# Seven block products for every output tile but the first, key folds on VectorE, split query transposes, one list for all steps

## The chip, the cores and the metric

The kernel runs on one core of a Trainium2 chip. The core's engines work side by side, each through its own queue in program order: TensorE multiplies matrices (PE in the profile; its weight loads are PEld), VectorE (DVE) and ScalarE (ACT) read TensorE's results from its accumulators in PSUM, GpSimd (POOL) folds arrays and issues the loads, SyncE (SP) issues stores and transposing DMAs. Sixteen DMA engines carry all transfers. The metric is the device time of one execution in microseconds, the median of several.

## What is computed

Attention over pooled keys and values, for 8 batches and 8 heads, followed by a three-way maxout layer and a projection.

```python
B, H, S, D = q.shape                      # 8, 8, 576, 64
pool = 8
Sp = S // pool                            # 72
k_p = k.reshape(B, H, Sp, pool, D).mean(axis=3)
v_p = v.reshape(B, H, Sp, pool, D).mean(axis=3)
scores = np.matmul(q, k_p.transpose(0, 1, 3, 2)) / np.sqrt(D)
attn = softmax(scores)                    # over the 72 pooled keys
x = matmul(attn, v_p).transpose(0, 2, 1, 3).reshape(B * S, H * D)   # 4608 x 512
h = np.maximum(np.maximum(x @ w1, x @ w2), x @ w3)                  # 4608 x 768
out = h @ w_out                                                     # 4608 x 512
```

## The kernel before

**Algebra.** The maximum is taken as x·w1 + max(0, x·(w2-w1), x·(w3-w1)). So the hidden layer has two products with difference weights (`sub_w`, line 331), and x·w1·w_out is one product with a 512x512 matrix `wm` made on the core (`turn_w`, `linear`, lines 338 to 355). An output tile then sums ten rows of 128 terms: four of `wm` with x, six of `w_out` with h.

**Tiles.** The 4608 tokens are cut into nine tiles of 512, numbered 0 to 8 (`NB`). A batch has 576 tokens, so tile n needs parts of one or two batches. For a batch b the steps are: load q, k, v (on POOL's queue, cast to 16 bits); fold eight keys into one and eight values into one; transpose queries (`qT`) and keys (`kz`); nine or eight score products with exponentials (`s`); five chunks of values (`v`: eight matmuls of 65 columns, a reciprocal and a multiplication on VectorE); five transposes of the normalised tokens into `xT` (`x`).

**Two ways to multiply.** A hidden or output tile is made directly (`hidden_part`, line 357, 48 matmuls of 512 columns; `project`, line 400, 40 of 512 columns), or as a 2x2 block product by seven instead of eight block products (`seven`, line 753, 84 matmuls of 256 columns; `out_seven`, line 643, 70 of 256). The seven need sums and differences of blocks of both operands (S1 to S4 of the weights, T1 to T4 of the tokens or hidden rows), and more than one eviction of each accumulator. The table `PRODUCTS` says which operands each of the products 1 to 7 takes. Before the change, hidden tiles 6, 7 and 8 and output tiles 2, 3, 4, 7 and 8 are made by seven products, the others directly.

**Order.** The program issues steps in an order written out by hand, and each engine's queue follows it. Three parts: `block(0, ...)`, line 810, runs tile 0's hidden layer, the product `wm` and tile 0's output, with batch 1's attention put into numbered slots. Then `MIDDLE` (line 881 and on) has a list for each of tiles 1 to 4: hidden pieces `h`, scores `s`, sums `a`, `b`, then output products, values and token transposes, with folds of the next batches on POOL (`k4+1`: one of three steps of batch 4's keys). After tile 5's hidden layer, `ORDER` (line 846) weaves the rest. Tile 8's output is made last, with the last pieces of tile 6's output behind it.

**Engines and queues.** Keys and values are folded on POOL in three additions each (`fold_steps`, lines 157 to 164; batch 0 by matmuls, batch 1's keys on VectorE). Queries of batches 3 to 7 are transposed by one DMA each on SP's queue (line 302), tokens of these batches by one DMA per chunk there (line 253); stores of the output use the same queue (lines 425 and 662). Batches 1 and 2 use TensorE for these transposes. A `!` in a list makes the next POOL fold wait for the last block sum on VectorE.

**PSUM.** In the first two parts two buffers of two banks (`att`) hold scores and values, three (`pw`) hidden and output products, one (`tr`) transposes. In the third part the tags are `val`, `sc`, `pa`, `bc` and `po`.

Of the kernel before, what the change touches and what calls it, by code (L numbers as in the profile page):

```python
# [14 lines left out]
def kernel(  # L15
# [26 lines left out]
    NG = 9  # L42
# [22 lines left out]
    kts, vts, qbs, kps, qTs, ets = {}, {}, {}, {}, {}, {}  # L65

# [15 lines left out]
    def load_v(b, eng, dtype=F16, cuts=(0, H)):  # L82
        if b == 0:
            vts[0] = ld.tile([96, 4096], dtype, name="vt0", tag="vt")[:, 0:3072].rearrange(
                "p (h i d) -> p h i d", h=H, i=6)
            src = v[0].rearrange("h (p i) d -> p h i d", i=6)
            return [eng.dma_start(out=vts[0][:, h:g], in_=src[:, h:g])
                    for h, g in zip(cuts, cuts[1:])][-1]
# [54 lines left out]
    vp_all = const.tile([Sp, B, H, 65], F16, name="vp", tag="vp")  # L143
# [10 lines left out]
    def fold(e, t, out, dtype=F32):  # L154
        return list(fold_steps(e, t, out, dtype))

    def fold_steps(e, t, out, dtype=F32):
        part, n = t.shape[:2]
        f = const.tile([part, n, 4, D], dtype, name="half" if dtype == F32 else "halfh",
                       tag="half" if dtype == F32 else "k16")  # L160
        yield e.tensor_tensor(out=f, in0=t[:, :, 0:4, :], in1=t[:, :, 4:8, :], op=ALU.add)  # L161
        yield e.tensor_tensor(out=f[:, :, 0:2, :], in0=f[:, :, 0:2, :],  # L162
                              in1=f[:, :, 2:4, :], op=ALU.add)
        yield e.tensor_tensor(out=out, in0=f[:, :, 0, :], in1=f[:, :, 1, :], op=ALU.add)

    def new_kp(b):
        kps[b] = sb2.tile([96, 6, D], BF16, name="kp", tag="kp")

    def fold_k(b, e, i0=0, i1=6):
        if b not in kps:  # L170
            new_kp(b)
        fold(e, kts[b][:, i0:i1], kps[b][:, i0:i1], F16 if e is nc.vector else F32)

    def fold_v(b):
        fold(nc.gpsimd, vts[b], vp_all[:, b, :, 0:D])

    def pool_v(b, h, g, tag, evac):

        pvp = psum([128, g - h, D], F32, name="pvp", tag=tag[0], bufs=tag[1])
        for i in range(6):  # L180
            nc.tensor.matmul(pvp, pick[:, i, :], vts[b][:, h:g, i, :],
                             start=(i == 0), stop=(i == 5))
        evac(out=vp_all[:, b, h:g, 0:D], in_=pvp[0:Sp])
# [12 lines left out]
    def keys(b, tag):  # L196
        pkt = psum([128, 3, 96], BF16, name="pkt", tag=tag[0], bufs=tag[1])
        for i in range(3):
            nc.tensor.transpose(pkt[:, i, :],
                                kps[b][:, 2 * i:2 * i + 2, :].rearrange("p i d -> p (i d)"),  # L200
                                ident[0:96, 0:96])
        return pkt

    def turn_k(b):
        pkt = keys(b, ATT if len(pools) < 3 else SC)
        for par, evac in enumerate((nc.vector.tensor_copy, nc.scalar.copy)):
            for odd in range(2):
                (evac if b > 2 else nc.vector.tensor_copy)(
# [55 lines left out]
    def values(b, c0):  # L264
        tag = (ATT0, ATT, ("val", 1))[len(pools) - 1]
        pav = psum([128, 2, 512], F32, name="pav", tag=tag[0], bufs=tag[1])
        for h in range(H):
            nc.tensor.matmul(  # L268
                pav[:, h // 4, 65 * (h % 4):65 * (h % 4) + 65],
                ets[b][:, h, c0:c0 + 128], vp_all[:, b, h, :],  # L270
# [20 lines left out]
    def do(b, steps):  # L291
# [3 lines left out]
        for name in steps.split():  # L295
            i = int(name[1:] or 0)
            if name[0] in "qQ":
                turn_q(b, *QS[i], nc.vector.tensor_copy if name[0] == "Q"
                       else nc.scalar.copy, TR)
            elif name[0] == "T":  # L300
                qTs[b] = sb2.tile([128, 2 * NG, 128], BF16, name="qT", tag="qT")
                nc.sync.dma_start_transpose(
                    out=qTs[b], in_=qbs[b].rearrange("p hp t d -> p (hp t d)"))
            elif name[0] == "k":
                turn_k(b)
            elif name[0] == "K":
                fold_k(b, nc.vector)
# [7 lines left out]
            elif name[0] == "S":  # L315
                next(out_sums, None)
# [7 lines left out]
            else:  # L324
                turn_x(b, *CHUNKS[i], xns[b, i], TR if b == 1 else ATT,
                       nc.vector.tensor_copy if name[0] == "X" else nc.scalar.copy)
# [73 lines left out]
    def project(n):  # L400
        hT = hTs[n]
        for mm in range(4):
            m = 4 * n + mm
            last = m == TOK // 128 - 9
# [3 lines left out]
            for c in ((slice(0, C // 2), slice(C // 2, C)) if last else (slice(0, C),)):  # L408
                tag = PW if len(pools) < 3 else PA if last else PO
                po = psum([128, c.stop - c.start], F32, name="po", tag=tag[0], bufs=tag[1])  # L410
                for kc in range(KCH):
                    nc.tensor.matmul(po, tokens(128 * m, 128 * m + 128)[:, kc], wm_sb[:, kc, c],  # L412
                                     start=(kc == 0), stop=False)
                yield
                for jc in (0, 3, 1, 4, 2, 5):
                    nc.tensor.matmul(po, hT[:, jc, bass.ts(mm, 128)], wo_sb[:, jc, c],  # L416
                                     start=False, stop=(jc == JCH - 1))
                if c.start:
                    nc.vector.tensor_copy(out=osb[:, c], in_=po)
                else:  # L420
                    nc.scalar.copy(out=osb[:, c], in_=po)  # L421
                for u in range(2):
                    b, g = divmod(2 * m + u, NG)
                    dst = out[S * b:S * b + S, :].rearrange("(r g) c -> r g c", g=NG)
                    (nc.scalar if last and u else nc.sync).dma_start(
                        out=dst[:, GS[g], c], in_=osb[64 * u:64 * u + 64, c])
# [90 lines left out]
    def block(n, plan, parts):  # L517

        for slot, _ in enumerate(part for stage in parts for part in stage(n)):
            for b, steps in plan.get(slot, ()):  # L520
                if b < B:
                    do(b, steps)
# [3 lines left out]
    PA, BC, PO = ("pa", 2), ("bc", 1), ("po", 1)  # L526
    FIRST = {1: (0, 0), 2: (1, 2), 7: ("S3", "T3")}
    PRODUCTS = FIRST | {3: ("S4", 3), 4: (3, "T4"), 5: ("S1", "T1"), 6: ("S2", "T2")}
    sw = {}

    LEAD = {0: [(6, "s0")], 1: [(6, "s1")], 2: [(6, "s2")], 3: [(6, "s3")],
            4: [(6, "s4")], 5: [(6, "s5")], 6: [(6, "s6")], 7: [(6, "s7")],
            8: [(6, "v0 x0")], 9: [(6, "v1 x1")]}

    def minus(out, a, b):
        gate[:] = [nc.vector.tensor_tensor(out=out, in0=a, in1=b, op=ALU.subtract)]

    def fold_w(wi):
# [3 lines left out]
        tag = ("w1T", "mw0")[wi - 1]  # L542
        s = const.tile([128, 4, 2, 128 * JH], F16, name=f"sw{wi}", tag=tag)
        sw[wi] = dict(zip(range(4), a)) | {f"S{i + 1}": s[:, i] for i in range(4)}
        nc.vector.tensor_tensor(out=s[:, 0], in0=a[2], in1=a[3], op=ALU.add)
        yield
        minus(s[:, 2], a[0], a[2])
        yield
        minus(s[:, 1], s[:, 0], a[0])
        yield  # L550
        minus(s[:, 3], a[1], s[:, 1])
        yield

    def halves(n):

        return {i: tokens(NB * n + HALF * (i % 2), NB * n + HALF * (i % 2) + HALF,
                          2 * (i // 2), 2 * (i // 2) + 2) for i in range(4)}

    def turns(n):
        return (pad3 if n % 2 else pad)[:, 0:4]  # L560

    def fold_t(e, x, t):
        for i, a, b in ((0, x[1], x[0]), (1, x[3], t[0]), (2, x[3], x[1]), (3, x[2], t[1])):
            e.tensor_tensor(out=t[i], in0=a, in1=b, op=ALU.subtract)  # L564

    def fold_x(n):

        x, t = halves(n), turns(n)
        late = n >= LAST - 1
        for part in ([slice(0, 1), slice(1, 2)] if late else [slice(0, 2)]):  # L570
            fold_t(nc.gpsimd if late else nc.vector,
                   {i: x[i][:, part] for i in x}, [t[:, i, part] for i in range(4)])
        return {f"T{i + 1}": t[:, i] for i in range(4)}

    LAST = TOK // NB - 1
    th, so_new, tt_all, gate, held = {}, [], [], [], []

    def out_w(z, r0, r1):

        i, j = divmod(z, 2)  # L580
        c = slice(HALF * i, HALF * i + HALF)
        return (wm_sb[:, 2 * j + r0:2 * j + r1, c] if r1 <= 2
                else wo_sb[:, JH * j + r0 - 2:JH * j + r1 - 2, c])

    def out_s(z):
        return so_new[0][:, z - 1]

    def fold_out(r0, r1):

        if not so_new:  # L590
            so_new.append(const.tile([128, 4, 5, HALF], F16, name="so", tag="ktTrue"))
        w = [out_w(z, r0, r1) for z in range(4)]
        t = [None] + [so_new[0][:, z, r0:r1] for z in range(4)]
        for out, x, y, op in ((t[1], w[2], w[3], ALU.add), (t[2], t[1], w[0], ALU.subtract),
                              (t[3], w[0], w[2], ALU.subtract),
                              (t[4], w[1], t[2], ALU.subtract)):
            gate[:] = [nc.vector.tensor_tensor(out=out, in0=x, in1=y, op=op)]
            yield

    out_sums = (x for rows in ((0, 2), (2, 5)) for x in fold_out(*rows))  # L600

    def sums_of(n, name):

        t = tt_all[0]
        h = name[0] == "b"
# [374 lines left out]
```

## Time and profile before

| what | value |
|---|---|
| median of 3 runs | 226.42 us (226.37 to 226.68) |
| the profiled execution: whole run | 228.01 us |
| the profiled execution: span from first to last instruction | 226.3 us |
| granted TensorE clock | 1.00 |
| DVE group L276, scaling of values, x40 | 27.7 us, 692 ns each |
| DVE group L769, maximum of two hidden halves, x18 | 13.3 us, 754 ns each |
| POOL group L161, first addition of values, x7 | 28.4 us, 4061 ns each |
| POOL group L161, first addition of keys, x6 | 18.7 us, 3125 ns each |
| DVE group L161, the same for batch 1's keys, x1 | 0.9 us, 947 ns |
| ACT group L208, copies of transposed keys, x10 | 4.8 us, 478 ns each |
| DMA queue of POOL, share of 16 engines | 48.1% |
| DMA queue of SP and ACT, share of 16 engines | 33.0% |

Busy time of an engine is the union of its instructions' durations. Matmuls overlap and their ends are modelled, so a busy TensorE can still lose time between instructions; the distance between starts of neighbouring pieces tells what one costs.

### The profile page before, as it was taken

What the parts mean: (1) busy time and instruction counts of PE and PEld (TensorE: products, weight loads), DVE (VectorE), ACT (ScalarE), POOL (GpSimd) and SP (SyncE); (2) the same over time, 40 slices, a digit from 0 to 9 for tenths busy, and PEclk for the clock granted to TensorE, in tenths of its full rate; (3) what the DMA queues carried; (4) which work ended last, traced back from release to release, by engine and by line L of the source; (5) the groups of instructions that cost most, each with busy time, mean ns of one, the idle gap of its engine ahead of it and who ended that gap; (6) DMA issues with size and microseconds to landing.
All of it is one profiled execution on the core that took longest, in us unless ns stands there. A gap on an engine that the chain in (4) does not pass through costs nothing.

```text
span 226.3 us, 4691 instructions
## 1 busy us (share of the span) xinstructions
PE 214.7 (95%) x1807; PEld 146.4 (65%) x1807; DVE 148.6 (66%) x292; ACT 122.3 (54%) x221; POOL 138.6 (61%) x111
## 2 busy tenths in 40 slices
PE   6788999999999999999999999699999999999993
PEld 2467745558656555965686568355677677788882
DVE  3668876038595385876679668535668886898840
ACT  2267524755874577238624862475687446555330
POOL 7974300999949967787677758999500913872020
PEclk9999999999999999999999999999999999999999
DMA  6999999989759999659999599965241534200265
GB/s 167 210 197 197 208 207 208 203 163 224 128 106 191 217 220 208 112 129 151 199 226 191 31 216 236 182 126 132 58 107 29 122 61 95 46 3 0 55 203 164
DMA packets 47351, 33.54 MB, mean 148 GB/s; under 512 B 27041, under 2 KB 42337, under 8 KB 47329
## 3 DMA queue, kind: packets, MB, share of 16 engines
q0 software_dynamic: 16944, 16.98, 48.1%
q1 hardware_dynamic: 29936, 15.87, 33.0%
q10 hardware_dynamic: 448, 0.39, 0.7%
q8 instruction: 14, 0.23, 0.5%
q14 instruction: 9, 0.07, 0.1%
HBM read 34.60 MB, written 9.44 MB: 195 GB/s over the span
## 4 chain that ended last, share of the span: by engine, by line
PE 69%; DMA 15%; POOL 11%; issue 1%; DVE 1%; ACT 1%; POOLq 0%
PE pw L362 21%; PE oA L713 9%; DMA vt<-in_v_dram 8%; PE pA L789 7%; PE po L416 7%; PE po L412 5%; PE oC L713 4%; PE psc L218 4%; DMA mw<-in_moe_w_dram 4%; PE pC L789 3%; POOL half L161 3%; DMA xT<-xn 3%; PE pav L268 3%; PE oB L713 2%; POOL half L162 2%; PE pB L789 2%
## 5 line engine op out<-in xcount | busy, mean ns | idle before, releaser
L362 PE MATMUL pw<-xT,mw 128*128 128x512 f16 (+1 forms) x336 | 72.8, 348 | 1.9 <-DMA xT<-xn 1.6
L362 PEld LDWEIGHTS <-mw 128*128 128x128 f16 x336 | 31.6, 98 | 22.3 <-DMA xT<-xn 1.8
L370 DVE TENSOR_TENSOR hT<-t,pw 128x512 f16<-128x512 f16 (+1 forms) x42 | 25.4, 609 | 25.1 <-ACT et L223 17.8
L223 ACT ACTIVATE et<-psc 72x576 f16<-72x576 f32 (+2 forms) x54 | 35.2, 661 | 6.8 <-PE psc L218 6.7
L161 POOL TENSOR_TENSOR half<-vt 72x2048 f32<-72x2048 f16 x7 | 28.4, 4061 | 13.8 <-DMA vt<-in_v_dram 13.3
L162 POOL TENSOR_TENSOR half<-half 72x1024 f32<-72x1024 f32 (+1 forms) x13 | 27.3, 2098 | 11.0 <-DVE rcp L274 6.1
L368 ACT ACTIVATE t<-pw 128x512 f16<-128x512 f32 (+1 forms) x42 | 22.5, 537 | 16.2 <-PE pw L362 15.8
L276 DVE TENSOR_TENSOR xn<-pav,rcp 128x512 f16<-128x512 f32 x40 | 27.7, 692 | 1.4
L416 PE MATMUL po<-mwo,hT 128*128 128x512 f16 (+1 forms) x102 | 23.5, 366 | 0.0
L218 PE MATMUL psc<-qT,kz 128*128 128x320 bf16 (+2 forms) x120 | 22.4, 278 | 0.8 <-DVE qT L194 0.6
L218 PEld LDWEIGHTS <-kz 128*128 128x128 bf16 x143 | 13.1, 98 | 13.3 <-ACT qT L194 1.1
L161 POOL TENSOR_TENSOR half<-ktFalse 96x1536 f32<-96x1536 f16 x6 | 18.7, 3125 | 4.0 <-issue 2.9
L564 POOL TENSOR_TENSOR pad<-xT 128x256 f16<-128x256 f16 x8 | 5.9, 732 | 22.5 <-ACT pad L795 13.9
L795 ACT CAST pad<-pA 128x512 f16<-128x512 f32 x27 | 15.6, 588 | 7.2 <-PE pA L789 7.0
L268 PEld LDWEIGHTS <-et 72*128 72x128 f16 x320 | 15.1, 98 | 3.6 <-issue 0.4
L723 ACT COPY osb<-oA 128x512 f32<-128x512 f32 x12 | 7.0, 586 | 19.2 <-PE oA L713 19.2
L274 DVE RECIPROCAL rcp<-pav 128x8 f32<-128x8 f32 x40 | 8.2, 204 | 14.0 <-PE pav L268 13.6
L412 PE MATMUL po<-wm,xT 128*128 128x512 f16 (+1 forms) x68 | 16.6, 366 | 0.0
L268 PE MATMUL pav<-vp,et 72*128 72x65 f16 x320 | 16.4, 194 | 0.1
L421 ACT COPY osb<-po 128x512 f32<-128x512 f32 (+1 forms) x16 | 9.2, 573 | 12.0 <-PE po L416 12.0
L789 PEld LDWEIGHTS <-sw 128*128 128x128 f16 x144 | 13.7, 98 | 2.5
L766 DVE TENSOR_TENSOR pad<-pad,pC 128x512 f16<-128x512 f16 x18 | 12.3, 685 | 3.9 <-PE pC L789 3.6
(122 smaller groups left out, 380.0 us busy)
## 6 DMA issues: line engine op xcount, KB each, us to landing
out_dram<-osb SPq DMA_DIRECT2D x38, 128.0 KB, 5.5
ktFalse<-in_k_dram POOLq DMA_DIRECT2D x7, 576.0 KB, 8.2
qb<-in_q_dram POOLq DMA_DIRECT2D x7, 576.0 KB, 13.0
vt<-in_v_dram POOLq DMA_DIRECT2D x7, 576.0 KB, 17.5
mw<-in_moe_w_dram POOLq DMA_DIRECT2D x9, 256.0 KB, 9.4
out_dram<-osb SPq DMA_DIRECT2D x8, 256.0 KB, 7.4
ktTrue<-in_k_dram SPq DMA_DIRECT2D x3, 384.0 KB, 5.2
out_dram<-ob SPq DMA_DIRECT2D x8, 128.0 KB, 2.6
```

Source lines behind the costliest of these rows:

```text
L161: yield e.tensor_tensor(out=f, in0=t[:, :, 0:4, :], in1=t[:, :, 4:8, :], op=ALU.add)
L162: yield e.tensor_tensor(out=f[:, :, 0:2, :], in0=f[:, :, 0:2, :], in1=f[:, :, 2:4, :], op=ALU.add)
L218: nc.tensor.matmul(out, kz_all[b % 2][f % 2][rows, h, :], qTs[b][rows, n + i0:n + i1, 64 * (h % 2):64 * (h % 2) + 64], start=True, stop=True)
L223: nc.scalar.activation(out=out, in_=in_, func=FT.Exp, scale=1.0 / 64.0)
L268: nc.tensor.matmul(pav[:, h // 4, 65 * (h % 4):65 * (h % 4) + 65], ets[b][:, h, c0:c0 + 128], vp_all[:, b, h, :], start=True, stop=True)
L276: nc.vector.tensor_tensor(out=xn, in0=pv[:, :, :, 0:D], in1=rcp.to_broadcast([128, 2, 4, D]), op=ALU.mult)
L362: mm = nc.tensor.matmul(pw, w_sb[wi][:, kc, bass.ts(jc, 128)], x[:, kc], start=(kc == 0), stop=(kc == KCH - 1))
L370: nc.vector.tensor_tensor(out=hT[:, jc, c0:c1], in0=t, in1=pw, op=ALU.max)
L412: nc.tensor.matmul(po, tokens(128 * m, 128 * m + 128)[:, kc], wm_sb[:, kc, c], start=(kc == 0), stop=False)
L416: nc.tensor.matmul(po, hT[:, jc, bass.ts(mm, 128)], wo_sb[:, jc, c], start=False, stop=(jc == JCH - 1))
L713: nc.tensor.matmul(p, left, right, stop=(r == 4), skip_group_check=True, start=(i in FIRST and r == 0 and (m == 0 or n == LAST)))
L789: mm = nc.tensor.matmul(p[:, w], a[:, kc, bass.ts(g, 128)], b[:, kc, :], start=(i in FIRST and w + kc == 0), stop=(w + kc == 2), skip_grou ...
```

## The change

**Output tiles.** Tiles 1 to 7 are made by `out_product`, which takes any of the seven products by itself; tile 8 by `out_last`; tile 0 stays direct (`project`). Hidden tiles 6, 7 and 8 stay with seven products (`hidden_product`), 1 to 5 direct (`two_products`; tile 1 in halves of 256 tokens).

**Product 1 and 2.** Before, product 1 was copied to SBUF and VectorE added product 2 to it. Now product 1 is copied from its bank A into a fresh bank B, product 2 is accumulated onto it by TensorE, and the result is read once. In the hidden layer the upper half of rows then takes a ReLU on ScalarE and a maximum on VectorE of 256 columns each.

**Evictions.** `move` puts a copy on ScalarE, or on VectorE where the step's name in the list has a `*`.

**Keys and values.** Keys of batches 1 to 7 are folded on VectorE in two additions to two halves `[96, 2, 6, D]`; the third addition is made by TensorE, which accumulates both halves in six matmuls with the identity in place of three transposes. Batch 1's values are pooled by twelve matmuls with `pick`; those of batches 2 to 7 on POOL in four pieces, then two, and a last addition on VectorE. Each POOL piece waits for the last instruction listed as `shared`, a sum on VectorE.

**Queries.** Each DMA transpose of queries is in three parts of six blocks.

**Sums.** All sums of tokens (`t`) and hidden rows (`u`) are on VectorE, in every tile that uses them. Before, those of tokens of tiles 7 and 8 and part of tile 7's hidden rows were on POOL.

**Scores and PSUM.** After the first block all scores are in nine pieces of 512 columns (`scores_flat`). Four single banks `pb0` to `pb3` are handed out in turn (`take`, `give`) to all hidden and output products; `sc` (2) holds scores and transposes, `val` (one buffer of two banks) the values.

**Order.** One list holds everything after tile 0's hidden layer and the weight product. Letters: `p` half a step of tile 0's output, `s31` score piece 1 of batch 3, `v31` and `x31` its value chunk and transpose, `T3` a third of its query transpose, `K3`, `V3` pieces of its folds, `<k3` a load, `A1` `A2` the two weight products of hidden row block A (of A, B, C, D, E, H) of the next direct tile, `A3` `A4` its two halves in tile 1, `1a` product 1 of hidden row group a of a seven-product tile, `1d` product 1 of an output tile, `t`, `u` block sums, `f` `F` `S` `G` weight sums, `k3` the transposed keys, `P0` pooling of batch 1's values.

```diff
+    def move(out, in_):
+        (nc.vector.tensor_copy if on_vector[0] else nc.scalar.copy)(out=out, in_=in_)
...
-        kps[b] = sb2.tile([96, 6, D], BF16, name="kp", tag="kp")
+        kps[b] = sb2.tile([96, 2, 6, D], F16, name="kp", tag="kp")
...
         for i in range(3):
-            nc.tensor.transpose(pkt[:, i, :],
-                                kps[b][:, 2 * i:2 * i + 2, :].rearrange("p i d -> p (i d)"),
-                                ident[0:96, 0:96])
+            for j in range(2):
+                nc.tensor.matmul(pkt[:, i, :], kps[b][:, j, 2 * i:2 * i + 2, :].rearrange("p i d -> p (i d)"),
+                                 identh[0:96, 0:96], start=(j == 0), stop=(j == 1))
...
                 nc.sync.dma_start_transpose(
-                    out=qTs[b], in_=qbs[b].rearrange("p hp t d -> p (hp t d)"))
+                    out=qTs[b][:, 6 * i:6 * i + 6],
+                    in_=qbs[b].rearrange("p hp t d -> p (hp t d)")[:, 768 * i:768 * i + 768])
...
+    free_banks = [0, 1, 2, 3]
+    taken = {}
+
+    def take(key, shape=(128, 2, 256)):
+        i = free_banks.pop(0)
+        taken[key] = i, psum(list(shape), F32, name="pb", tag=f"pb{i}", bufs=1)
+        return taken[key][1]
+
+    def give(key):
+        free_banks.append(taken.pop(key)[0])
...
+    def hidden_product(n, i, g):
...
+        if i == 1:
+            move(out=bank("B", n, g), in_=p)
+        elif i in (6, 5):
+            move(out=y[:, i == 5], in_=p)
+        elif i in (2, 3):
+            t0 = sb2.tile([128, NB], F16, name="t0", tag="t0")[:, 0:HALF]
+            nc.scalar.activation(out=t0, in_=p[:, 0], func=FT.Relu)
+            nc.vector.tensor_tensor(out=h_of(g)[:, i - 2], in0=t0, in1=p[:, 1], op=ALU.max)
+        if i in (5, 7) and (n, 12 - i, g) in done:
+            plus(1)
+        if i == 4:
+            plus(0)
+            shared[:] = [nc.vector.scalar_tensor_tensor(
+                out=h_of(g + JH), in0=y[:, :, 0], scalar=0.0, in1=y[:, :, 1],
+                op0=ALU.max, op1=ALU.max)]
...
+    def out_product(n, i):
+
+        p = bank(of(i), n, "d")
+        for r in range(5):
+            for m in range(2):
+                nc.tensor.matmul(p[:, m], *out_operands(n, i, m, r), stop=(r == 4),
+                                 start=(i in (1, 7) and r + m == 0), skip_group_check=True)
...
+        if i == 1:
+            move(out=bank("B", n, "d"), in_=p)
+        elif i != 4 and i != 7:
+            move(out=o(int(i in (5, 3)))[:, :, lo if i in (2, 3) else hi], in_=p)
...
+        f = const.tile([Sp, H, 4, D], F32, name="half", tag="half")
+        e = nc.gpsimd
+        for i in range(0, H, 2):
+            c = slice(i, i + 2)
+            yield e.tensor_tensor(out=f[:, c], in0=t[:, c, 0:4, :], in1=t[:, c, 4:8, :],
+                                  op=ALU.add)
...
+        gate = shared[0]
+        op = next(folding[what, b])
+        if op is not None and gate is not None:
+            after([op], gate)
...
+    ORDER = """
+        q10* k1 p q11* q12* P0 q13* s10 K2 <k3 s11 p* s12 s13 <k4 p s14 P1 s15 V2 s16 s17 K2
+        s18 p v10 q20 q21* p k2 V2 f G v11 x10* p* v12 V2 V2 <v3 K3 G x11 s20 <q3 p q22 v13
+        K3 F s21 p* s22 s23 D3 V2 s24 q23* C3 V2 x13 K4 <q4 T3 V2 x12 A3 S v14 s25 t1 s26 F
+        C4 s27 s28 B4 k3 v20 x14 B3 E4 v21 K4 x20 t2 H3 A4 x21 v22 E3 V3 H4 k4 T3 x22* v23
+        <k5 V3 V3 t1 T4 D4 T3 F B1 u1 V3 S B2 t3 s30 s31 H1 s32 G V3 v24 s33 H2 u3 C1 C2 <k6
+        1d* V3 s40 K5 S G <v4 u2 s41 S <q5 T4 A1 s34 A2 f s35 E1 s36 T4 s37 V3 6d* u4 s38 E2
+        s42 K5 s43 K6 5d* u1 v30 s44 x23 2d x24* s45 D1 v31 f k5 s46 V4 3d t2 v32 K6 7d t4
+        s47 s48 T5 v33 D2 k6 <q6 t3 4d V4 1d t1 V4 D1 T5 T5 u2 D2 t4 V4 V4 v34 V4 E1 6d* C1
...
+        4b 5d 4a 1c 3d 6c* t1 7d u4 5c t2 2c 7c 3c 4d 1a v72 4c 6a u1 1b 2a 5a v73 6b u2 2b
+        3a t3 5b v74 1d u4 u3 3b 7a 6d t4 2d* 1c 4a 5d* 2c t1 6c 7d t2 7b t3 3d* 4d 5c 4b 1a
+        3c 7c 2a 6a 1b 4c t4 5a 6b 7a 2b 3a 5b 4a u1 1d 3b 7b 2d 1c u2 u3 4b 6d* 6c 2c u4 7c
+        5c 5d* 3c 7d 4c 3d 4d
+    """
+
+    run(ORDER)
+    last = out_last(LAST)
+    for i in range(4):
+        sum_h(LAST, i)
```

More of the change, by code (lines that the diff above doesn't have):

```diff
@@ L559, in turns @@
[L559 to L573, printed above, removed]
@@ new lines, in fold_out @@
+    def fold_out(h, e):
+        if h:
+            s = const.tile([128, 4, JH, HALF], F16, name="soh", tag="w1T")
+        else:
+            s = sums[:, 3072:5120].rearrange("p (i k c) -> p i k c", i=4, k=2)
+        so[h] = s
+        w = [out_w(z, h) for z in range(4)]
+        yield both(s[:, 0], w[2], w[3], ALU.add, e)
+        yield both(s[:, 2], w[0], w[2], ALU.subtract, e)
+        yield both(s[:, 1], s[:, 0], w[0], ALU.subtract, e)
+        yield both(s[:, 3], w[1], s[:, 1], ALU.subtract, e)
```

667 lines of the change are left out of this document (276 added, 391 removed), and 3 rows, old and new, of the table stop.

## The prediction

> **What bounds the kernel now.** I read four views: the page's busy row and slices, busy time by stretch, the chain of waits, and single groups. TensorE first.
>
> ```profile
> PE 214.7 (95%) x1807; PEld 146.4 (65%) x1807; DVE 148.6 (66%) x292; ACT 122.3 (54%) x221; POOL 138.6 (61%) x111
> ...
> PE   6788999999999999999999999699999999999993
> ```
>
> PE is busy 95% of the span. Its slices fall only in the first 20 us, in slice 26 (141 to 147 us) and in the last slice. By stretch (length, then busy us and instructions of PE, PEld, DVE, ACT, POOL, then clock, DMA share, GB/s):
>
> ```profile
> 57.00:78.00 21.00, 20.86 (x167) 12.11 (x165) 12.19 (x25) 13.54 (x26) 17.66 (x10) 1.00 0.83 158
> 78.00:99.50 21.50, 21.35 (x177) 14.49 (x176) 15.81 (x33) 11.97 (x21) 16.16 (x10) 1.00 0.90 163
> 121.00:143.00 22.00, 21.44 (x179) 14.27 (x177) 16.19 (x34) 11.61 (x20) 15.56 (x10) 1.00 1.16 162
> 143.00:158.50 15.50, 13.91 (x93) 7.52 (x91) 6.81 (x13) 9.26 (x16) 14.95 (x8) 1.00 0.77 149
> 158.50:180.00 21.50, 21.50 (x197) 15.36 (x195) 16.00 (x32) 14.56 (x28) 7.41 (x8) 1.00 0.34 73
> 180.00:200.00 20.00, 20.00 (x169) 15.23 (x168) 15.88 (x25) 11.09 (x21) 9.38 (x14) 1.00 0.32 68
> 222.00:226.30 4.30, 0.49 (x5) 0.20 (x2) 0.42 (x1) 0.00 (x0) 0.00 (x0) 0.99 0.51 141
> ```
>
> The part that is already one woven list (158.5 on) has no idle PE; the part by stages (36 to 158.5) loses a little in each and 1.6 us in one place. The chain of waits (start, length, what) names that place:
>
> ```profile
> 137.42 1.09 PE oC L713 x10
> 138.71 6.32 DMA xT<-xn
> 145.17 1.02 PE pw L362 x4
> ```
>
> TensorE waits for transposed tokens. In the timeline, SP's queue holds two token transposes from 137.3, then one whole query transpose (4.94 us from 140.08), and only then three more. Two rows matter later: the time from issue to landing of the 27 token transposes, and a vector subtraction (min/median/max ns) that once took 1348.
>
> ```profile
> DMA to landing us min/median/max: 2.3/2.7/11.8
> ```
>
> ```profile
> L597 DVE TENSOR_TENSOR so<-wm x2: 417/882/1348, 62.3 to 64.0; 128x512 f16<-128x512 f16 x2
> ```
>
> So TensorE's own work, plus what it loses between 37 and 158, sets the time.
>
> **Work moved on or off TensorE.** From starts of neighbouring pieces in the chain: a 512-column matmul costs 0.2165 us (four in 0.86), a 256-column one 0.109 (ten in 1.09), eight value matmuls 0.27 (sixteen are busy 0.69, eight 0.42). An output tile done directly is 40 x 0.2165 = 8.66 us, by seven products 70 x 0.109 = 7.63. Tiles 1, 5 and 6 change over: 3 x -1.03 = **-3.1**. Keys go from 3 transposes to 6 matmuls in each of 7 batches: 21 x 0.042 (three pkt are busy 0.29, of which some 0.165 is the tail of the last) = **+0.9**. Values of batch 1 go through twelve `pick` matmuls instead of GpSimd: 12 x 0.109 = **+1.3**. Scores change their cut, not their columns: 0. Net **-0.9 us**.
>
> **Waits that the list could remove.** From 37.7 (end of the weight product) to 158.3 lie 120.6 us. Counted by kind: hidden layers of tiles 1 to 5, 216 x 0.2165 + 48 x 0.109 = 52.0; tiles 0 and 1 out, 17.3; tiles 2 to 4 out, 22.9; scores of six batches at 1.95, 11.7; 27 value steps, 7.3; query, key and token transposes, 4.8. Together 116.0, so **4.6 us** are lost there; the windows show 2.9 of it as idle, and the rest hides under modelled ends of matmuls. The new list starts attention of batches 1 and 2 beside tile 0's output, and puts other products between each wait and its user. The split query transposes stop one 4.9 us block from holding token transposes. Upper bound of this gain 4.6, lower bound 0.
>
> **What else moves, at no cost while PE covers it.** DVE: sums of tokens and hidden rows, now in all eight tiles, 32 x 0.42 + 32 x 0.557 = 31.3 against 16.6 now, +14.6. Key folds 6 x (0.947 + 0.555), rows of batch 1's fold, +9.0. Last step of six value folds, +2.5 (0.42 each, as other 512-element f16 adds). Sixteen output and two hidden evictions put on DVE, 18 x 0.687, +12.4; three of tile 0 and nine query and token copies, less two of now, +5. Two more output adds +1.6. Key copies to ACT -8.6. Hidden products -5.0: per group five DVE passes of 0.69 to 0.75 become three of these and two 256-column maxima of 0.416, because product 1 is written into a second bank and product 2 accumulates on it. In all about +31, so 149 becomes 180 of some 223 us. GpSimd falls from 139 to some 66: 24 x 1.03 + 12 x 1.19 for folds (4.06/4 and 2.35/2), 25 for loads, the rest set-up. ACT stays near 122: -18 evictions, +13.4 key copies, more hidden passes.
>
> DVE is the cover to distrust. Over the last four full lines of the list (about 155 to 204 us) I count 49.1 us of DVE durations beside 49.1 of PE. But a DVE instruction that doesn't read its forerunner starts about 0.084 before that one's end (subtractions of 0.55 start every 0.47 in the timeline at 134.92); with that it is 42.8, or 87%, and 97% in the worst line. It fits, with little slack: no cost in the sum, up to +1.5 in the range.
>
> At the start of the list DVE meets the fold of batch 2's keys, whose load landed at 45.1; the copy of tile 0's first output, the second fold and batch 1's value steps queue behind it. From 45.1 to the end of line 3 DVE has 2.2 + 7.1 + 6.3 = 15.6 us to do (overlapped starts), which ends at 60.7; PE's own work reaches that point at 58.1. Line 4 asks 7.3 of DVE beside 9.9 of PE, so DVE catches up there. PE waits only where a value step needs the bank that DVE has not read (the second and third of batch 1, by this walk): 0.5 us in all, part of the new waits below. POOL's loads leave in the old order up to 25 us, later ones earlier than now (batch 5's keys near 62, against 78.9), each as its buffer comes free. SP carries 15 query transposes in place of 5; whole ones took 1.95 to 5.5 us there, so thirds should take 0.7 to 1.8; SP is empty more than half the time.
>
> [...] The subtraction of 1348 ns started at 62.28, while GpSimd added from 62.08 to 63.34; the same form alone takes 417. [...] More such DVE instructions (some 70 against 44 while GpSimd folds) run beside shorter GpSimd pieces. [...] If each of 36 pieces held up one sum by half its 1.1 us, DVE would gain 20 us: its 91 us on lines 1 to 14 (102.6 of durations, less the 0.084 where starts overlap) would be 111 beside 117 of PE. [...]
>
> **The end.** Now PE stops at 222.5, then one 0.42 copy and two 64 KB stores on two queues, 3.8 us. After, the last vector add is followed by two 128 KB stores on SP: some 0.5 later, from 2.6 (128 KB) against 2.1 to 2.3 (64 KB) to land: **+0.5**; bounds 0 and 1.
>
> **New waits.** Bounds: 0, as in the woven stretch of before, and 7.6 (rival 2). I take **+2.0**, the rate of the steady stage, whose repeat of 21.72 us holds 21.45 of counted work: 0.27 in 21.7, over 180 us of list 2.2; the 0.5 of the early loads is in it.
>
> **Sum.** 226.3 - 0.9 - 4.6 + 0.5 + 2.0 = 223.3 of span. The median of runs, 226.42, is 0.1 above the span (the profiled run itself took 228.01 with what lies around it): **223.4 us**, own range 221.2 (no new wait) to 225.3.
>
> **Rivals.**
> [...]
> 2. *Token transposes land late: slower.* 18 of 27 landed in 2.3 to 3.7 us, nine took 4.2 to 11.8, all with loads of k, q, v in flight. The tightest place in the list is tile 3's first product (first D1 of that tile): 5.1 us of PE work lie between the value step v32 and it. The step's two vector passes take 0.93, so the transpose must land within 4.2 of issue. At the median of the slow nine (8.0) PE waits 3.8, at 11.8 it waits 7.6: 227.2, up to 231. Against: the loads before it are listed some 12 us earlier and should have landed.
> 3. *Nothing is won back*: the 4.6 us are lost again in other places, at the early loads and in the DVE-full end: 226.3 - 0.9 + 0.5 + 0.5 = 226.4. It costs the same as rival 1 and shares its chance.
>
> **Chances.** Forecast 0.61, rivals 1 and 3 together 0.14, rival 2 0.25. A difference under 0.2%, 0.45 us, can't be told from none here. The forecast lies wholly below 225.97; of the 0.14 I put 0.03 faster, 0.08 same, 0.03 slower; rival 2 slower. So faster 0.64, same 0.08, slower 0.28. The range takes in the list without waits and part of rival 2: 220.8 to 228.6.
>
> **What would show it.** Right: PE busy near 214 of a span of 223; no PE stall over 1 us between 40 and 215; no token transpose on the chain ahead of tile 3; POOL near 66, DVE near 175. Wrong: sums with medians over 0.5 us (rival 1); a DMA xT<-xn piece of several us in the chain (rival 2); ACT or PE waiting on DVE after 155 (the DVE count); PE idle around 40 to 60 above 1.5 us (early loads).

## The result, and the profile after

| what | before | after |
|---|---|---|
| median, device us | 226.55 | 235.44 (234.32 to 237.28) |
| ratio, with its 95% interval | 1 | 1.040 (1.030 to 1.050) |
| profiled span | 226.3 | 234.7 |
| last matmul ends | 222.5 | 230.2 |
| granted clock, mean | 1.00 | 0.993 |

The change makes the kernel 4.0% slower; 223.4 us and a faster kernel were forecast. The busy rows and slices of the page after (each digit is the busy share of a fortieth of the span, in tenths):

```profile
PE 216.5 (92%) x1985; PEld 161.0 (69%) x1986; DVE 171.4 (73%) x353; ACT 121.5 (52%) x238; POOL 73.5 (31%) x84
...
PE   7787998999999999679997969999999999999992
...
PEclk9999999999999999979999999999999999999999
```

PE's work is not what grew: 216.5 us busy against 214.7, with part of that at a lower clock. New are three holes, in slices 17, 22 and 24 of 40 (digits 6, 7 and 6; these slices begin at 94, 123 and 135 us), with the clock down in slice 18, behind the first. The windows of the changed kernel (bounds, length, busy us and instructions of PE, PEld, DVE, ACT, POOL, then clock, DMA share, GB/s) say when:

```profile
80.00:100.00 20.00, 17.60 (x179) 13.47 (x177) 15.99 (x33) 15.02 (x29) 5.13 (x6) 1.00 0.94 141
100.00:120.00 20.00, 18.76 (x155) 12.55 (x156) 12.50 (x26) 7.76 (x14) 9.61 (x9) 0.91 0.93 150
120.00:140.00 20.00, 16.26 (x129) 9.79 (x127) 12.56 (x25) 8.31 (x15) 7.57 (x9) 1.00 0.99 173
140.00:160.00 20.00, 20.00 (x190) 14.60 (x189) 15.27 (x30) 10.21 (x21) 10.34 (x9) 1.00 0.89 152
...
101.00:103.00 2.00, 1.76 (x6) 0.76 (x7) 0.90 (x2) 0.43 (x1) 1.27 (x1) 0.71 1.14 336
103.00:105.00 2.00, 2.00 (x13) 0.97 (x12) 0.65 (x2) 0.17 (x1) 0.13 (x1) 0.50 0.88 195
...
200.00:222.00 22.00, 22.00 (x202) 19.49 (x200) 19.75 (x37) 9.90 (x21) 0.00 (x0) 1.00 0.21 50
```

From 140 to 222 TensorE is never idle, not even where VectorE is 90% busy (19.75 of 22). The chain of waits (start, length, what) names all three holes:

```profile
92.78 0.69 DVE xn L268
...
93.50 7.60 DMA xT<-xn
...
101.24 3.00 PE pb L664 x8
...
117.06 7.37 DMA qT<-qb
...
124.46 0.33 PE psf L210 x2
...
128.93 8.18 DMA qT<-qb
...
137.16 0.49 PE psf L210 x4
```

Each is a transposing DMA that takes 7 to 8 us. The timeline of TensorE puts the stop behind each in brackets: 3.64, 1.31 and 2.43 us.

```profile
101.24 3.00 PE L664 MATMUL pb<-xT,mw 128*128 128x512 f16 x8 [3.64 <-DMA xT<-xn]
124.46 0.33 PE L210 MATMUL psf<-qT,kz 128*128 128x320 bf16 x2 [1.31 <-DMA qT<-qb]
137.16 0.49 PE L210 MATMUL psf<-qT,kz 128*128 128x256 bf16 x4 [2.43 <-DMA qT<-qb]
```

With no load in flight, 15 token transposes of this kernel landed 2.3 to 4.8 us after issue, their median 2.4, and four thirds of query transposes 2.8 to 4.5. The timeline of POOL's queue shows what left beside the first:

```profile
93.41 0.77 POOL L104 DMA_DIRECT2D qb<-in_q_dram  x1
```

Load q6 landed at 101.28, the two parts of the token transpose at 101.10 and 101.45. The second hole is T6's middle third (117.06 to 124.42) beside load k7 (117.27 to 123.63); the third is its last third (128.93 to 137.12) beside v6 (129.13 to 138.39) and q7.

**Where the time went.** The forecast's own sum puts the last matmul, without any waits, at 222.5 - 0.9 - 4.6 = 217.0. At the prices of the prediction I walked the list and took, for each step of TensorE, its start in the trace less the list's work before it. This *lag* creeps up by 0.4 us in each of the two long stretches without such a wait, so its jumps are the losses:

| place | us |
|---|---|
| start of the list to s17 (q12 +0.75, s10 +0.38, s17 +0.39) | 2.8 |
| from there to v32 | 0.4 |
| first D1 of tile 3 waits for tokens | 3.8 |
| lower clock behind it | 1.6 |
| T6, middle third | 1.5 |
| T6, last third | 2.6 |
| from 140 to the end | 0.4 |
| sum, lag of the last matmul | 13.1 |

The forecast allowed 2.0 of it. The rest, 11.1, and a tail of 4.6 instead of 4.3 make up 234.7 - 223.3 = 11.4.

### The profile page after: what moved, and what is told of

It is laid out like the page before. It is cut to its first block, busy times and chain, and to the rows that moved or that the text cites. A ratio compares the mean times of both kernels' runs of the same rounds, so it can differ in the third digit from the quotient of the medians.

```text
span 234.7 us, 5073 instructions
## 1 busy us (share of the span) xinstructions
PE 216.5 (92%) x1985; PEld 161.0 (69%) x1986; DVE 171.4 (73%) x353; ACT 121.5 (52%) x238; POOL 73.5 (31%) x84
## 4 chain that ended last, share of the span: by engine, by line
PE 74%; DMA 14%; DVE 5%; ACT 2%; issue 1%; POOL 1%; SPq 1%; POOLq 0%; DVEq 0%
PE pb L706 19%; PE pb L664 14%; PE pb L615 12%; DMA qT<-qb 7%; PE psf L210 5%; PE pb L655 4%; PE pw L352 4%; DMA vt<-in_v_dram 4%; PE pav L260 3%; DMA xT<-xn 3%; PE pb L747 2%; PE pm L339 2%; PE pb L403 2%; DVE xn L268 2%; PE pxt L251 1%
## 5 line engine op out<-in xcount | busy, mean ns | idle before, releaser
L664 PE MATMUL pb<-xT,mw 128*128 128x512 f16 x192 | 48.3, 388 | 3.6 <-DMA xT<-xn 3.6
L796 POOL TENSOR_TENSOR half<-vt 72x512 f32<-72x512 f16 x24 | 28.3, 1193 | 53.5 <-DVE xs L526 19.4
L215 ACT ACTIVATE et<-psf 72x512 f16<-72x512 f32 x63 | 34.7, 588 | 19.4 <-PE psf L210 19.3
L664 PEld LDWEIGHTS <-mw 128*128 128x128 f16 x192 | 18.1, 99 | 20.2 <-issue 5.3
L671 DVE TENSOR_TENSOR hT<-t,pb 128x512 f16<-128x512 f16 (+1 forms) x36 | 21.2, 595 | 12.4 <-PE pb L664 9.8
L669 ACT ACTIVATE t<-pb 128x512 f16<-128x512 f32 (+1 forms) x36 | 18.7, 526 | 21.5 <-PE pb L664 15.8
L210 PE MATMUL psf<-qT,kz 128*128 128x256 bf16 (+4 forms) x161 | 21.6, 249 | 4.4 <-DMA qT<-qb 3.7
L210 PEld LDWEIGHTS <-kz 128*128 128x128 bf16 x185 | 14.2, 97 | 10.7 <-issue 5.3
L800 POOL TENSOR_TENSOR vt<-half 72x512 f16<-72x512 f32 x12 | 15.0, 1262 | 12.6 <-DVE hs L526 6.0
L706 PEld LDWEIGHTS <-hs 128*128 128x128 f16 x168 | 16.4, 98 | 1.9
L266 DVE RECIPROCAL rcp<-pav 128x8 f32<-128x8 f32 x40 | 8.1, 202 | 12.7 <-PE pav L260 12.6
L706 PE MATMUL pb<-soh,hs 128*128 128x256 f16 x126 | 17.2, 273 | 0.0
```

What stands on the lines that cost most here:

```text
L210: nc.tensor.matmul(out, kz_all[b % 2][f % 2][rows, h, :], qTs[b][rows, n + i0:n + i1, 64 * (h % 2):64 * (h % 2) + 64], start=True, stop=True)
L215: nc.scalar.activation(out=out, in_=in_, func=FT.Exp, scale=1.0 / 64.0)
L664: nc.tensor.matmul(a, w_sb[part + 1][:, kc, bass.ts(j, 128)], tokens(NB * n, NB * n + NB)[:, kc], start=(kc == 0), stop=(kc == KCH - 1))
L669: nc.scalar.activation(out=relus[j], in_=a, func=FT.Relu)
L671: nc.vector.tensor_tensor(out=hTs[n][:, j, c], in0=relus[j], in1=b, op=ALU.max)
L706: nc.tensor.matmul(p[:, m], *out_operands(n, i, m, r), stop=(r == 4), start=(i in (1, 7) and r + m == 0), skip_group_check=True)
```

## The experiments

The theory: a transposing DMA that is issued while loads are in flight lands with them, and the new list has too little work between such a transpose and its user. Rivals: the split of the query transposes alone, or the list itself (engines, copies, PSUM banks). All runs start from the changed kernel unless said otherwise; ratios are to the kernel before.

**1. One late load moved, one group of transposes moved, both** (e1, e2, e3).

```diff
# e1_q6_later
-        s47 s48 T5 v33 D2 k6 <q6 t3 4d V4 1d t1 V4 D1 T5 T5 u2 D2 t4 V4 V4 v34 V4 E1 6d* C1
+        s47 s48 T5 v33 D2 k6 t3 4d V4 1d t1 V4 D1 T5 T5 u2 D2 t4 V4 V4 v34 V4 <q6 E1 6d* C1
# e2_t6_early (the two later T6 are taken out)
-        ... u3 V5 v40 T6 2d* u4 ...
+        ... u3 V5 T6 T6 T6 v40 2d* u4 ...
```

> The changed kernel with one load moved: batch 6's queries are listed behind the sixth piece of batch 4's value fold instead of ahead of its second. Theory (a token transpose issued beside a 576 KB load lands with the load): the two transposes that tile 3's first product needs land within 4 us of issue instead of 7.6; the 3.8 us wait ahead of that product goes, and with it the stretch of lower granted clock behind it (1.6 us): about 5.4 us less, 230.0 us. Rival (SP's queue or the transposing itself is slow there, whatever POOL loads): the wait stays, 235.4 us.

> The changed kernel with batch 6's three query transposes listed together ahead of value step v40, none behind it. Theory: their two waits (1.5 us at score piece s62, 2.6 us at s64 and s65), each behind a transpose issued within 0.2 us of a load, go: 4.1 us less, 231.3 us. Rival (the waits only move to the token transposes that now stand behind the three on SP's queue): 235 us, with TensorE waiting for xT<-xn around tile 4.

> Both edits of the two runs beside this one. Theory: the gains add, 5.4 + 4.1 = 9.5 us less, 226 us, level with the kernel before, and no wait over 1 us for a transposing DMA. Rival (one wait hides another): less than 7 us gained, 228.5 us or more.

Measured: e1 238.92 us, 1.050 (1.043 to 1.057); e2 233.75, 1.027 (1.019 to 1.034); e3 237.15, 1.046 (1.041 to 1.051). All three totals missed: e1 and e3 by 9 and 11 us, e2 by 2.4 (its profiled execution, 231.46, is the shortest of its four). In e1 the wait at D1 is gone: the same transposes left at 93.77 and 94.99 and landed 2.3 us later. But T5's middle third (104.00 to 110.81) now met q6, and its last third, issued at 105.55, met q6 and v5 and landed with v5 at 118.2; TensorE stopped 3.5 and 3.7 us for them, and the granted clock of that execution averaged 0.969, against 0.993 of the changed kernel's. The long DMA at that place in e1's chain, and in e3's:

```profile
105.55 12.69 DMA qT<-qb
```

```profile
104.36 11.45 DMA qT<-qb
```

In e2 the two waits for T6 are gone as expected, and the last matmul ends at 225.0 instead of 230.2, the earliest of the three. Yet T6's thirds met a load again: issued at 108.40, 109.67 and 111.66 beside v5 (108.22 to 116.62), they took 7.8 to 8.4 us, only now TensorE did not wait for them. In e1 and e3 a load moved off one transpose lands on the next.

**2. TensorE kept busy through the wait** (e4): sixteen matmuls of 512 columns ahead of D1, whose product nobody reads.

```diff
-        ... 1d t1 V4 D1 T5 T5 u2 ...
+        ... 1d t1 V4 W16 D1 T5 T5 u2 ...
```

> The changed kernel with 16 more matmuls of 512 columns on constants, 3.5 us of work, where TensorE idles ahead of tile 3's first product; their result is used nowhere. Theory (the granted clock falls because TensorE idled for 3.6 us): the clock stays at 1.00 there, the following products run at their usual 0.2165 us, and the kernel is 1.6 us faster in spite of more work: 233.8 us. Rival (the clock falls for another reason): same time or up to 3.5 us more, the clock still low after 101 us.

Measured: 242.2 us, 1.064 (1.056 to 1.071). In the profiled execution, at 244.55 us the longest of four, T6's last third fell on loads v6 and q7 later on (11 us); what lengthened the other three is not shown. But at D1 the question is answered, by the windows of e4 at that place:

```profile
100.00:102.00 2.00, 1.35 (x7) 0.50 (x6) 0.30 (x1) 0.00 (x0) 0.00 (x0) 1.00 0.37 127
102.00:104.00 2.00, 2.00 (x18) 1.05 (x17) 0.89 (x3) 0.60 (x1) 1.40 (x1) 1.00 1.17 290
```

The clock stays at 1.00, where the changed kernel showed 0.71 and 0.50; the lag grows by 4.3 there and no more, against 3.8 + 1.6. So the 1.6 us at this place are the clock's answer to the stop of 3.64 us. In e2 it stood at 0.50 too, from 101 to 103 us, behind a stop of 2.18:

```profile
98.00:100.00 2.00, 0.00 (x0) 0.01 (x1) 0.00 (x0) 0.50 (x1) 0.11 (x1) 1.00 1.21 235
100.00:102.00 2.00, 1.98 (x6) 0.74 (x7) 0.89 (x2) 0.20 (x1) 1.39 (x1) 0.54 1.16 316
102.00:104.00 2.00, 2.00 (x14) 1.04 (x13) 0.42 (x1) 0.39 (x1) 0.00 (x0) 0.60 1.22 93
```

**3. Load q6 first; then the keys of batch 1 on the other engine** (e5, e6).

```diff
# e5_q6_first, with e2's edit; <q6 taken out of its old place
-        ... s36 T4 s37 V3 6d* u4 ...
+        ... s36 T4 s37 <q6 V3 6d* u4 ...
# e6_k1_vector, on top of e5
-        q10* k1 p q11* q12* P0 q13* ...
+        q10* k1* p q11* q12* P0 q13* ...
```

> The changed kernel with batch 6's queries loaded about 11 us earlier (listed before batch 4's value fold, right after the last query transpose of batch 4, so that nothing loads beside token transposes x32 and x33 or the last thirds of batch 5's queries), and batch 6's three query transposes listed together ahead of v40. Theory (a transposing DMA issued while loads are in flight lands with the last of them): all three waits and the lower clock go, 235.4 - 3.8 - 1.6 - 4.1 = 225.9 us, a shade under the kernel before. Rival (such waits turn up elsewhere whatever is moved, because the DMA queues are full at that stage): 231 us or more.

> The run beside it, and the four copies of batch 1's transposed keys on VectorE instead of ScalarE. Theory (ahead of 47 us ScalarE, with four key copies and then exponentials, holds up TensorE: 0.75 us at q12, 0.4 at s10, 0.4 at s17): 1.2 to 1.5 us less than the run beside it, 224.5 us. Rival (the wait there is for loads): no change.

Measured: e5 235.04 us, 1.037 (1.034 to 1.039): D1 loses 0.5 instead of 3.8, and T5 meets v5 (issued 104.47) for 5.8 at s53. That is the rival of its expectation, by its time and by the wait elsewhere; that the queues are full there is not shown. e6 235.83, 1.043 (1.040 to 1.046): nothing gained. q12 waits for a PSUM bank that four key copies hold for 1.95 us on ScalarE (e5) and 1.94 on VectorE (e6).

**4. The parts alone, in the kernel before** (e7, e8).

```diff
# e7_before_split: query transposes in three parts between the token transposes
-            1 v0 x0 2 v1 x1 6:T 6 7 v2 x2 5 v3 x3 v4 x4 3 4
+            1 v0 x0 2 v1 x1 6:T0 6 7 v2 x2 6:T1 5 v3 x3 6:T2 v4 x4 3 4
# e8_before_v7: load v7 behind the token transpose that waited at 145
-            h k k7< q7< v7< h ...    1 v0 x0 2 v1 x1 7:T ...
+            h k k7< q7< h ...        1 v0 x0 2 v1 x1 v7< 7:T ...
```

> The kernel before with one part of the change alone: query transposes in three parts, with token transposes between the thirds. Reading of the prediction (one 4.9 us block on SP's queue holds the tokens for which TensorE waits at 145): 1.5 us less, 224.9 us. Rival (those two token transposes were issued ahead of the block, at 137.3 and 138.7, and landed with the load of batch 7's values, 144.2): no change, 226.5 us.

> The kernel before with the load of batch 7's values listed behind the second token transpose of batch 5 instead of ahead of all, the rest unchanged. Theory (transposes land with the loads in flight): the two transposes land 2.5 us after issue, the wait at 145 goes, 1.5 us less, 224.9 us. Reading of the prediction (the block of the query transpose): no change, 226.5 us.

Measured: e7 took 227.7 us in one run and 233.8 to 234.4 in three, so its ratio stays open; the profile, of one of the three, shows TensorE stopped for tokens (96.60 to 103.36) that met load v5 (80.99 to 102.36), 4.5 us and some 2.6 more at a lower clock (0.84 on average from 99.5 to 121). T5's last third, issued at 106.14 beside q6, landed only at 117.52, but TensorE did not wait for it. None of the four is below the kernel before, so no gain of the split alone is seen. e8: 227.45, 1.003 (1.002 to 1.005). The two token transposes landed in 4.1 and 3.2 us instead of 7.3 and 6.3, so load v7 made that wait, not the query transpose behind them. Between the two profiled executions the last matmul moves from 222.5 to 221.4. The median gains nothing: the execution of the kernel before that was profiled, 228.01 us, is 1.6 longer than the median, and whether the others had this wait at all is not shown.

**5. The split undone** (e9): each query transpose whole, where its first third was listed.

```diff
-                nc.sync.dma_start_transpose(
-                    out=qTs[b][:, 6 * i:6 * i + 6],
-                    in_=qbs[b].rearrange("p hp t d -> p (hp t d)")[:, 768 * i:768 * i + 768])
+                    nc.sync.dma_start_transpose(
+                        out=qTs[b], in_=qbs[b].rearrange("p hp t d -> p (hp t d)"))
```

> The changed kernel with each query transpose whole again, at the place where its first part is listed; everything else as changed. Theory (a transposing DMA that is issued beside a load lands with the load, so later parts have more chances to meet one): the two waits for the last parts of batch 6's queries (+1.5 and +2.6 us in the changed kernel) go, the wait of 3.8 us for tile 3's tokens and the lower clock behind it (+1.6) stay, so 235.4 - 4.1 = 231.3. Rival (it is the list's DMA traffic, not the parts): the whole transposes meet loads as the parts did, or hold the token transposes behind them by some 5 us, and the time stays at 234 to 238.

Measured: 233.97 us, 1.031 (1.027 to 1.035), at the lower edge of the rival. So the parts are not the whole cause. In the profiled execution, at 239.11 us the longest of four, the waits for T6 are gone, but batch 4's transpose, whole, left at 70.18, met a load of keys (70.36 to 80.80) and landed at 85.32; s40 lost 5.7. Whether the other three lost this too is not shown.

**6. Every transpose of batches 3 to 6 away from the loads as they stood** (e10), with batch 1's key copies shared by two engines (e11).

```diff
# e10_clear_of_loads, on top of e5
-        ... 3d t2 v32 K6 7d t4 / s47 s48 T5 v33 ... V4 D1 T5 T5 u2 ...
+        ... 3d t2 v32 T5 T5 T5 K6 7d t4 / s47 s48 v33 ... V4 D1 u2 ...
# e11_keys_two_engines, in turn_k
-                move(
+                (nc.vector.tensor_copy if b == 1 and odd else move)(
```

> The changed kernel with every transpose of batches 3 to 6 put where no load is in flight: load q6 right after batch 4's last part, the three parts of batch 5's queries directly after step v32, the three parts of batch 6's ahead of v40. Theory: of the 13.1 us that the changed kernel lost behind its list's own PE work, only the early 2.7, some 0.5 at tile 3 and 0.4 late are left, so the span is 217.1 + 3.6 + 4.5 = 225.2 and the time some 226 (225 to 228), level with before. Rival (the list leaves no room, waits turn up elsewhere as in the runs so far): 231 or more.

> The same with batch 1's four serial key copies shared between ScalarE and VectorE, two each. Theory (query part q12 waits for the PSUM bank that the four copies hold for 1.94 us): the hold halves and 0.75 us of the early loss goes, 0.6 to 0.8 us below the run beside it, so some 225.3. Rival: VectorE is busy with the query copies then, and the loss stays (no change within 0.3).

Measured: e10 235.52 us, 1.040 (1.035 to 1.044). Nothing is lost at D1, at s53 or for T6; the one wait over 1 us that is left is new, tile 4's tokens beside load k7 (114.68 to 121.09), 4.4 us and 2.6 more at half clock (0.50 from 122 to 126). From e10's chain:

```profile
116.02 6.07 DMA xT<-xn
```

e11 234.60, 1.037 (1.034 to 1.041), no different. It did not test its theory: the four copies still ran one after another, ACT, DVE, ACT, DVE (38.30 to 40.31), each released by the one before.

**7. No late loads at all, in both kernels; one more order** (e12 to e15). e12 and e15 keep every step and leave out loads; e13 moves k7 behind s63 in e10; e14 lists q11 ahead of k1 in e13.

```diff
# e12_no_late_loads (k from 7, q from 6, v from 5); e15_before_no_late_loads the same from batch 6
     def load_q(b):
+        if b > 5:
+            qbs[b] = qbs[5]
+            return
# e13_clear_k7
-        ... v41 s54 <k7 t3 s55 V5 B1 / s56 ... H2 u1 s63 / V5 B2 A1 ...
+        ... v41 s54 t3 s55 V5 B1 / s56 ... H2 u1 s63 / <k7 V5 B2 A1 ...
# e14_query_first
-        q10* k1 p q11* q12* P0 q13* ...
+        q10* q11* k1 p q12* P0 q13* ...
```

> The changed kernel without the six loads that it issues from 93 us on (q6, v5, k7, v6, q7, v7): batches 5 to 7 use the tile of the last batch that is loaded, so the outputs of those batches are those of other inputs; every step and its place stay. Theory (transposing DMAs land late because loads are in flight): all of the waits at tile 3 and for batch 6's queries go, with the lower clock behind them, 3.8 + 1.6 + 1.5 + 2.6 = 9.5 us, so 235.4 - 9.5 = 225.9 (225 to 227). Rival (the list itself, its copies and its order on the engines): most of the loss stays, 232 or more.

> e10_clear_of_loads with load k7 moved behind step s63, past tile 4's tokens, whose transposes landed with it there (B1 +4.4 us, then +3.0 at a lower clock). Theory: those 7.4 us go and 3.3 + 0.6 of lag are left: span 225.3, time 226 to 228. Rival: some other transposes meet k7 in its new place, 231 or more.

> e13_clear_k7 with q11 listed ahead of k1, so that q12 takes the PSUM bank that q11's copy has freed and not the one that the four key copies hold. Theory: 0.75 us of the early lag goes, 0.5 to 0.8 below the run beside it. Rival: P0 waits for the keys' bank in q12's place, and the time stays within 0.3.

> The kernel before without the loads of batches 6 and 7, which it issues from 100 us on (batch 5's tiles are used again, so the outputs of those batches are those of other inputs). Theory: its own waits for transposes beside loads (some 1.6 us at 145, and what it loses to others) go: 224.5 to 225.5, so that without late loads the two kernels are within some 1.5 us of each other, against 9 with them. Rival: it gains as much as the changed kernel (over 5 us), and then loads aren't what sets the two apart.

| run | median us | ratio (95%) | profiled span |
|---|---|---|---|
| e12, changed, no late loads | 228.58 | 1.008 (1.005 to 1.011) | 226.3 |
| e13, one more order | 230.65 | 1.020 (1.015 to 1.025) | 228.1 |
| e14, q11 first | 232.08 | 1.023 (1.018 to 1.029) | 229.3 |
| e15, before, no late loads | 226.99 | 1.002 (0.999 to 1.004) | 225.5 |

This settles the main cause, the late loads. Six loads fewer, in the same list, are worth 235.44 - 228.58 = 6.9 us (8.4 by the profiled spans) to the changed kernel. Those of batches 6 and 7 are worth nothing that can be measured to the kernel before. The page of e12 has no hole behind the first block, and its chain no long DMA but one query transpose:

```profile
PE 215.1 (95%) x1986; PEld 160.6 (71%) x1986; DVE 172.2 (76%) x353; ACT 121.2 (54%) x238; POOL 69.4 (31%) x78
...
PE   7887999899999999998999999999999999999991
```

```profile
103.96 3.81 DMA qT<-qb
```

It is not that the kernel before avoids the loads. The DMA view of 93 to 140 us gives count and median us from issue to landing of the token transposes; before, after, and e12:

```profile
xT<-xn SPq DMA_TRANSPOSE x13, 6.3
```

```profile
xT<-xn SPq DMA_TRANSPOSE x11, 3.7
```

```profile
xT<-xn SPq DMA_TRANSPOSE x14, 2.4
```

The kernel before has the slowest transposes of the three and pays little for them: one stop, the 1.6 us at 145. Its stages issue them long before use: T5 to T7 at 98.9, 117.8 and 140.1, with the first scores of these batches at 124.6, 146.0 and 161.9, that is 22 to 28 us. Two token transposes issued at 101.1 and 102.4 took 10.7 and 11.8 us, and TensorE did not wait. In the new list T6's last third was issued 5.7 us before TensorE was ready to read it (128.93, 134.7), and tile 3's tokens 2.7 to 3.9 (93.50 and 94.73, 97.4). For T6 run e2 shows that this distance decides: issued 6 to 17 us sooner, its thirds still took some 8 us beside a load, and the waits were gone. For the other places it is read from the traces; no run changed it alone there. e13 is the fastest order found, 4.8 us under the changed kernel, but 2.0% over the kernel before: the waits at D1, at s53, for T6 and beside k7 are gone, and the next two, 1.4 us for tile 4's tokens and 1.3 for tile 5's, have come up. So an order gets back about half of the loss; none was found that beats the kernel before. Nor would the new list without late loads: e12 is 1.6 us above e15.

e14 gained nothing: by the timelines of PE in e13 and e14, the wait for the keys' bank only changes its owner, from q12 to P0, as its rival said. Its median is 1.4 us above e13's, outside the rival's 0.3; the runs of the two overlap (230.3 to 233.7 and 230.0 to 233.1).

```profile
40.42 0.38 PE L184 MATMUL pqt<-ident,qb 128*128 128x128 bf16 x4 [0.59 <-ACT kz L69]
```

```profile
41.13 0.81 PE L173 MATMUL pvp<-vt,pick 96*128 96x256 f16 x6 [0.94 <-ACT kz L69]
```

## Why the prediction was wrong, point by point

- **The step that failed is "New waits", +2.0 us.** It took the rate of a steady stage, 0.27 us in 21.7. The list's waits are not a rate: the large ones are each a transpose that meets a load. Measured 13.1 in all. Without late loads 4.7 are left (the lag of the last matmul in e12), so some 8.4 are the loads' and 2.7 of the miss are not.
- **Rival 2 was the mechanism.** It named the place, tile 3's first D1 behind v32, and its price at the median slow transpose, 3.8 us; measured 3.80. That the two agree so closely is luck: the transposes landed in 7.6 and 6.7 us, not 8.0, and TensorE was ready 3.9 and 2.7 us after their issue, not 4.2. It was given 0.25 because "the loads before it are listed some 12 us earlier and should have landed". That overlooked the load listed *behind* v32. POOL's queue takes no notice of TensorE's place in the list: POOL reached `<q6` as soon as it was free, at 93.41, 0.1 us ahead of the transpose. Even so it stopped at one place. The same sum for each query part, with its distance to its reader, would have pointed at T6's two waits; and the clock that a stop takes down was left out. Its 227.2 "up to 231" was short for that.
- **"The split query transposes stop one 4.9 us block from holding token transposes": a wrong reading.** The wait at 145 was load v7 (e8). No gain of the split as such was seen (e7), and undoing it did not cure (e9).
- **The gain of 4.6: the old waits went, but even without late loads nothing is left of it.** Between its jumps the lag creeps by 0.4 us in a long stretch, so the work was priced nearly rightly and the steady places lose little. But in e12 the lag is still 4.7, and e12 is 1.6 us slower than e15. So rival 3 (the 4.6 are lost again in other places) holds for what is left once the late loads are gone.
- **From span to time, +0.1: a wrong reading.** The span of 226.3 belongs to an execution of 228.01 us, the span after, 234.7, to one of 236.44: 1.7 apart each time. A median of 226.42 goes with a span near 224.7. So a span of 223.3 means some 225.0 us, under half of the gain forecast, and 1.6 of what was counted in the profiled execution need not be there in most others.
- **PE's work, -0.9: not contradicted.** PE is busy 214.5 to 215.1 in e13 and e12, where the clock is nearly full (0.998 in both), against 214.7 before and "near 214" expected. Busy time, with its modelled ends, can't show 0.9; the nearly flat lag speaks for the count. The excess to 216.5 after is put down to the lower clock (0.71 and 0.50 in the windows from 101 to 105), an estimate of the author's.
- **VectorE: right that it costs nothing, counted too high.** 171.4 us against a count of 180 ("near 175" in the signs to look for); the full lines after 155 lose nothing. Sums held up beside GpSimd's folds decided nothing: the longest, 768 elements, average 608 ns against 557, some 0.8 us in sixteen. No run shows the 20 us of such delay that stood behind part of the 0.14 for rivals 1 and 3, nor what stretched the one row of 1348 ns. GpSimd has 73.5 against 66, ScalarE 121.5 against 122.
- **The early part: mis-sized and misplaced.** 0.5 us was taken, for value steps behind the fold of k2. Measured 2.8, half of it at q12, s10 and s17, which wait until ScalarE has read one of the two `sc` banks. It is most of the lag of 4.7 that e12 still has.
- **The end, +0.5: within its bounds** (4.6 against 3.8, +0.8).

## What to carry to other kernels

For a DMA that an engine will wait for, count the work between its issue and its reader, and compare it with the landing time beside a load, not alone; here 6.1 to 12.7 us against 2.4. A hand-written list orders the steps of one engine, but the queue of another can run ahead of it, so a load "listed later" can leave first: here q6, listed behind v32, left at 93.41, the token transpose of v32 at 93.50. Before moving one transfer out of the way of another, look at what it will meet next: four of the orders tried here only moved the wait, and a run without the loads told in one look how much was to be had.

## What the runs showed of the hardware

- The transposing DMAs beside a 576 KB load in the chain lines above landed 6.1 to 12.7 us from issue, in the changed kernel, e1 and e10 within 1.3 us of a load's landing, where token transposes take 2.4 without loads (e12). Others differ: in the changed kernel a token transpose issued at 115.79, 1.5 us ahead of load k7 (117.27 to 123.63), took 3.7, and in e9 the whole query transpose at 70.18 took 15.1 and landed 4.5 us behind the load of keys. What holds them is not shown by any run here.
- The clock dropped to 0.5 with stops of TensorE of 2.18 (e2), 3.64 (the changed kernel) and 4.24 us (e10), and not after 1.31 and 2.43 (the changed kernel), so the length alone does not decide. The price is 1.6 to 2.6 us beyond the stop itself.
- Four copies from one PSUM tile into two SBUF tiles, given to two engines by turns, still ran one by one, 0.5 us each, each released by the one before (e11). Whether the program or the chip orders them so is not shown.
